# Holding the x transposes back behind the first chunk, in a one-core gated mix of linear attention and an MLP

## Chip, cores and metric

One core of one Trainium2 chip. The metric is device time in microseconds (us), the median of five runs. TensorE does the matmuls into PSUM, VectorE (DVE) and ScalarE (ACT) evacuate PSUM and do elementwise work, GpSimd (POOL) does masks and small copies, and SyncE (SP) issues nearly all DMAs.

## The reference

`x` is 2048 tokens by 640 features, everything is bfloat16. One input `x` goes through two blocks, and a gate for each token mixes the results:

```python
g = sigmoid((x * gate_w).sum(-1, keepdims=True))
# A: linear attention, H = 32 heads of 20
q, k, v = heads(x @ wqkv)
pq, pk = phi(q), phi(k)                  # phi(t) = where(t > 0, t + 1, exp(t)) + 1e-6
kv, z = einsum(pk, v), pk.sum(over s)    # for each head
a = (pq @ kv) / (pq . z + 1e-6) @ wo
# B: shifted mixer and MLP
h = gelu(layernorm(x) @ w1)
x1 = x + shifted(h) @ w2                 # four column groups, shifted by 1, -1, 2, -2 tokens
b = x1 + gelu(layernorm(x1) @ w3) @ w4   # 640 -> 1728 -> 640
out = g * a + (1 - g) * b
```

## The kernel before, in words

The instructions are written in a fixed order (`tc.manual_schedule()`): each engine runs its own instructions in program order, waiting on semaphores where data or buffers require it. A DMA instruction reuses one of eight DMA semaphores in turn, so it also waits until the DMA eight before it has landed. PSUM is handed out as four pairs of banks (`pair()`), in turn.

Tokens lie in 16 chunks of 128 (`NCH`) and 4 tiles of 512 (`NT`); 640 features are 5 groups of 128 (`DC`). TensorE's stages are, in order: K (L187, for each chunk 5 feature groups by 2 halves, 10 matmuls), q (L244), g (L321, k against x), W1 for tiles 0 and 1 with the small attention matrices between (L355, L374, L259, L388), W2 of tile 0 (L437), W1 of tiles 2 and 3, and then for each tile W3 (L484) with the next tile's W2 (L437) and this tile's attention (L468) woven in, followed by W4 (L517), whose sums go out with L531 and L536.

**The start.** K needs `xT`, which is x with features on partitions, and `wk_sb`, the weight rows for K. Loads go out on two queues, SP's and ACT's (L129 to L136): x chunk 0, the gate vector, K's weight rows 1, 0, 3, 2, 4 and x chunk 1. Chunks 0 and 1 are transposed on TensorE by `turn(c)` (L209 to L223): matmuls against an identity into PSUM, and then copies to `xT` on DVE (L220). The transposes of chunk 0 come in two groups, features 0 and 1, then 2 to 4. A column for the gate is made the same way (L219, L223) and sits as column 640 of `wk_sb`. Chunks 2 to 15 of `xT` come by DMA transposes from DRAM, written right behind the weight loads on SP's queue (L137, L138; `load_xT`, L124), in pieces of 1, 1, 2, 2, 4 and 4 chunks. After them, on the same queue: the weights for q (L139), the rest of x (L140, L141), the weights for v (L142), w1 (L143), six pieces of wo (L145), w2 in eight pieces (L147, L148) and w3 (L149).

While nothing has arrived, TensorE runs matmuls on constants ("fillers", `warmup`, L200). Chunk 0 of K takes the feature groups in the order 1, 0, 3, 4, 2 (`k0_order`), with a filler of 256 columns before the second and the third, and `turn(1)` before the fourth (L227 to L232). The copies of L171 (GpSimd, 20 of them) build `w1x` out of `w1_sb`.

**Scaling q.** `scale_t(t)` (L278 to L280) multiplies tile t of `pqT`, the 5 x 512 columns of phi(q), by the reciprocal denominators `rb`, on DVE. It needs `rb` (four DMAs, L276), and the attention matmuls of that tile (L468) need it. Tiles 0 and 1 are scaled before W1 of tile 3 in DVE's order, tiles 2 and 3 after it (L589 to L594).

**W4.** `w4_tile(t)` (L547) runs W4's matmuls of token chunks 0 and 2, then the rest rows and W3's rest of the next tile, then chunks 1 and 3; DVE adds the results up (L531) and SP stores them.

Of the kernel before, what the change touches and what calls it, by code (L numbers as in the profile page):

```python
# [16 lines left out]
def kernel(  # L17
# [13 lines left out]
    nc = tc.nc  # L31
    P = 128
    S, D = A_x.shape[1], A_x.shape[2]
# [6 lines left out]
    DC = D // P  # L40
# [4 lines left out]
    CG = D // 4  # L45
# [4 lines left out]
    NG = 6  # L50
    row0 = [g * GW for g in range(5)] + [D - P]
# [5 lines left out]
    wqkv_v = A_wqkv.rearrange("(c p) f -> p c f", p=P)  # L57
# [13 lines left out]
    def pair():  # L71
        return ps.tile([P, 2, 512], F32, name="pp")
# [5 lines left out]
    w1_sb = const.tile([P, DC, D], BF16)  # L78
    w1x = const.tile([P, DC, P], BF16)
    w2_sb = const.tile([P, DC, D], BF16)  # L80
    w3_sb = const.tile([P, DC, F], BF16)
    wo_sb = const.tile([P, NG, D], BF16)
# [22 lines left out]
    wq_sb = hsT[:, :, 0:D]  # L105
    wv_sb = m_sb
# [5 lines left out]
    xT = st1.tile([P, DC, S], BF16)  # L112
# [5 lines left out]
    sp, aq, gq = nc.sync, nc.scalar, nc.gpsimd  # L118

    def load_x(c0, c1, q=sp):  # L120
        q.dma_start(x_sb[:, c0:c1, 0:D], x2[c0 * P:c1 * P, :].rearrange("(c p) d -> p c d", p=P))  # L121

    def load_xT(c0, c1):
        sp.dma_start_transpose(xT[:, :, c0 * P:c1 * P], x2[c0 * P:c1 * P, :])  # L124

    def load_wk(q, dc):
        q.dma_start(wk_sb[:, dc, 0:D], A_wqkv[dc * P:(dc + 1) * P, D:2 * D])  # L127
# [6 lines left out]
    load_wk(sp, 3)  # L134
    load_wk(aq, 2)
    load_wk(sp, 4)  # L136
    for c0, c1 in ((2, 3), (3, 4), (4, 6), (6, 8), (8, 12), (12, 16)):  # L137
        load_xT(c0, c1)  # L138
    sp.dma_start(wq_sb, wqkv_v[:, :, 0:D])  # L139
    load_x(2, 8)  # L140
    load_x(8, 16)  # L141
    sp.dma_start(wv_sb[:], wqkv_v[:, :, 2 * D:3 * D])  # L142
    sp.dma_start(w1_sb[:], B_w1.rearrange("(c p) f -> p c f", p=P))  # L143
    for g in range(NG):
        sp.dma_start(wo_sb[:, g, :], A_wo[row0[g]:row0[g] + P, :])  # L145
    for g in range(4):
        sp.dma_start(w2_sb[:, g, :], B_w2[CG * g:CG * g + P, :])  # L147
        sp.dma_start(w2_sb[32 * g:32 * (g + 1), 4, :], B_w2[CG * g + P:CG * (g + 1), :])  # L148
    sp.dma_start(w3_sb[:], B_w3.rearrange("(c p) f -> p c f", p=P))  # L149


    nc.gpsimd.memset(mhalf[:], -0.5)
# [10 lines left out]
    for m, n, off in ((bmask, GH, 0), (bmask5, 2, 88)):  # L163
# [2 lines left out]
                                base=-off, pattern=[[-Dh, n], [0, 4]], channel_multiplier=1)  # L166
        nc.gpsimd.affine_select(out=m[:], in_=m[:], compare_op=ALU.is_ge, fill=0.0,
                                base=off + Dh - 1, pattern=[[Dh, n], [0, 4]], channel_multiplier=-1)
    for dc in range(DC):
        for g in range(4):  # L170
            nc.gpsimd.tensor_copy(w1x[:, dc, 32 * g:32 * (g + 1)], w1_sb[:, dc, CG * g + P:CG * (g + 1)])  # L171


    def phi(dst, src, n):
# [8 lines left out]
    def k_mm(pt, c, dcs, first=0, last=DC - 1):  # L183
        for dc in dcs:
            for hf in range(2):
                n = HD + hf
                nc.tensor.matmul(pt[:, hf, 0:n], lhsT=xT[:, dc, c * P:(c + 1) * P],  # L187
                                 rhs=wk_sb[:, dc, hf * HD:hf * HD + n], start=(dc == first), stop=(dc == last))
# [9 lines left out]
    def warmup(n, w=TS):  # L198
        for i in range(n):
            nc.tensor.matmul(warm[:, 1, 0:w], lhsT=one[:, 0:P], rhs=one[:, 0:w], start=True, stop=True)  # L200
# [8 lines left out]
    def turn(c):  # L209
        for pt, a, b in turns:  # L210
            ptb = pt[:, 0, :].bitcast(BF16) if c else pt[:, 0, :]
            for dc in range(a, b):
                dst, src = ptb[:, (dc - a) * P:(dc - a + 1) * P], x_sb[:, c, dc * P:(dc + 1) * P]
                if c:
                    nc.tensor.transpose(dst, src, ident[:])
                else:
                    nc.tensor.matmul(dst, lhsT=src, rhs=ident[:], start=True, stop=True)
            if c == 0 and b == DC:
                nc.tensor.matmul(pt[:, 1, 0:DC], lhsT=g5z[:], rhs=ident[:, 0:DC], start=True, stop=True)  # L219
            nc.vector.tensor_copy(xT[:, a:b, c * P:(c + 1) * P],  # L220
                                  ptb[:, 0:(b - a) * P].rearrange("p (c s) -> p c s", c=b - a))
            if c == 0 and b == DC:
                nc.vector.tensor_copy(wk_sb[:, :, D], pt[:, 1, 0:DC])  # L223

    turn(0)
    warmup(1, TS)
    for n, dc in enumerate(k0_order):  # L227
        if n == 3:
            turn(1)
        elif 1 <= n < 3:  # L230
            warmup(1, 2 * P)
        k_mm(kp, 0, (dc,), first=k0_order[0], last=k0_order[-1])  # L232
    k_evac(kp, 0)
    for c in range(1, NCH):
# [43 lines left out]
    def scale_t(t):  # L278
        sl = pqT[:, :, t * TS:(t + 1) * TS]
        nc.vector.tensor_tensor(sl, sl, rb[:, t:t + 1, :].broadcast_to([P, DC, TS]), op=ALU.mult)  # L280
# [177 lines left out]
    def x1_scale(t, cc):  # L458
        c = t * CPT + cc
        x1 = st[t]["x1"][cc]  # L460
        nc.scalar.activation(x1[:], x1[:], ACT.Copy, scale=omg[:, c:c + 1])
# [27 lines left out]
    def w3_rest(t, dst):  # L489
        for dc in range(DC):  # L490
            for v in range(2):
                nc.tensor.matmul(dst[FR * v:FR * (v + 1), :], lhsT=w3_sb[:, dc, FF * P:F],  # L492
                                 rhs=st[t]["lnT"][:, dc, v * LT:(v + 1) * LT], start=(dc == 0), stop=(dc == DC - 1))
        st[t]["h2x"] = h2x_p.tile([P, LT], BF16, name="h2x")
        nc.scalar.activation(st[t]["h2x"][:], dst, ACT.Gelu_apprx_tanh)  # L495
# [3 lines left out]
    def w4_tiles(t, ccs, pts):  # L499
        if t < NT - 1:  # L500
            for cc in ccs:
                pt = pair()
                pts[cc, 0], pts[cc, 1] = (pt[:, 0, TS - LT:TS], 0, LT), (pt[:, 1, 0:D - LT], LT, D)
                pts[cc, "rest"] = pt[:, 0, 0:LT]
                pts[cc] = pt[:].rearrange("p h e -> p (h e)")[:, TS - LT:TS - LT + D]
        else:
            for _ in range(3 if 0 in ccs else 1):
                pts["pairs"] = pts.get("pairs", []) + [pair()]
            homes = {0: (0, 1), 2: (1, 2)} if 0 in ccs else {1: (3, 3), 3: (2, 0)}
            for cc, (w, n) in homes.items():  # L510
                wide, narrow = pts["pairs"][w][:, 0, :], pts["pairs"][n][:, 1, 0:NW]
                pts[cc, 0], pts[cc, 1] = (narrow, 0, NW), (wide, NW, D)

    def w4_mm(t, cc, pts, hf, start):
        dst, a, b = pts[cc, hf]
        for fc in range(FF):
            nc.tensor.matmul(dst, lhsT=st[t]["h2"][:, fc * TS + cc * P:fc * TS + (cc + 1) * P],  # L517
                             rhs=w4_sb[:, fc, a:b], start=start and fc == 0, stop=not start and fc == FF - 1)

    def w4_rest(t, pts):  # L520
        for u in range(2):
            for hf in range(2):
                for v in range(2):
                    rows = slice(FR * v, FR * (v + 1))
                    dst, a, b = pts[u + 2 * v, hf]
                    nc.tensor.matmul(dst, lhsT=st[t]["h2x"][rows, u * P:(u + 1) * P],  # L526
                                     rhs=w4_sb[rows, FF, a:b], start=u == 1, stop=u == 0)
# [10 lines left out]
    def w4_out(t, cc, pts):  # L538
        oc = outp.tile([P, D], BF16, name="oc")
        if t < NT - 1:  # L540
            w4_stt(t, cc, oc, pts[cc], 0, D)
        else:
            for hf in range(2):
                w4_stt(t, cc, oc, *pts[cc, hf])
        w4_store(t, cc, oc, 0, D)

    def w4_tile(t):  # L547
        last = t == NT - 1
        pts = {}
        w4_tiles(t, (0, 2), pts)  # L550
        for cc in (0, 2):
            if not last:
                x1_scale(t + 1, cc)
            for hf in (1, 0):
                w4_mm(t, cc, pts, hf, True)
        w4_tiles(t, (1, 3), pts)
        w4_rest(t, pts)
        if not last:
            w3_rest(t + 1, pts[0, "rest"])
        for cc in (0, 2):  # L560
            w4_out(t, cc, pts)
        ocs = {}
        for cc, hf in ((1, 1), (3, 1), (1, 0), (3, 0)) if last else ((1, 0), (1, 1), (3, 0), (3, 1)):
            if not last and hf == 0:
                x1_scale(t + 1, cc)
            w4_mm(t, cc, pts, hf, False)
            if last:
                if hf == 1:
                    ocs[cc] = outp.tile([P, D], BF16, name="oc")
                w4_stt(t, cc, ocs[cc], *pts[cc, hf])  # L570
                w4_store(t, cc, ocs[cc], *pts[cc, hf][1:])
            elif hf == 1:
                w4_out(t, cc, pts)
# [13 lines left out]
    nc.sync.dma_start(w4_sb[0:FR, FF, :], B_w4[FF * P:F, :])  # L587
    nc.sync.dma_start(w4_sb[FR:P, FF, :], B_w4[FF * P:F, :])
    scale_t(0)  # L589
    scale_t(1)  # L590
    for fcs in w1_split:
        w1_unit(3, fcs)
    scale_t(2)
    scale_t(3)  # L594
    for cc in range(CPT):
        x1_scale(0, cc)
    NW3 = (FF + 1) // 2
# [45 lines left out]
```

## Time and profile before

| | us |
|---|---|
| median of five runs | 263.57 (263.08 to 266.35) |
| the profiled execution's own time | 263.57 |
| its span, first to last instruction | 261.9 |
| busy: TensorE | 257.5 |
| busy: DVE, ACT, GpSimd | 142.0, 83.0, 18.7 |
| K's unbroken run of matmuls starts | 6.66 |
| q starts | 27.80 |
| last output add starts | 259.19 |

The profile is of one execution; the times in it count from the span's start. "Busy" of TensorE is the union of its matmuls, whose ends are modelled. The chain of waits is followed back from the last instruction; each step in it is what the next one waited for. A row of a timeline gives start, length, engine, line, operation, output and inputs, and in brackets the idle time before it with what ended it. An issue on SP ("SPq") lasts as long as SP is busy with it; the data land later.

### The profile page before, as it was taken

To read this page: it belongs to the slowest core of one execution; us is meant where nothing else is said; L and a number is where in the kernel's file an instruction comes from. 1 tells how busy PE (TensorE), PEld (TensorE's weight loads), DVE (VectorE), ACT (ScalarE), POOL (GpSimd) and SP (SyncE) were. 2 spreads that over 40 slices of the span, in tenths; PEclk is the share of its full clock that TensorE was granted. 3 is DMA by queue.
4 is the path that set the end of the run, shared out by engine and by line. 5 is a ranking of instruction groups with operands and counts; after the bars stand their busy time and mean duration, and the time that the engine had idled before them with its cause. 6 is when DMAs were issued, how large, how long until landed. Compare 5 with 4: busy or idle time off the path is not lost.

```text
span 261.9 us, 4141 instructions
## 1 busy us (share of the span) xinstructions
PE 257.5 (98%) x1670; PEld 158.7 (61%) x1670; DVE 142.0 (54%) x277; ACT 83.0 (32%) x124; POOL 18.7 (7%) x64
## 2 busy tenths in 40 slices
PE   7999999999999999999999999999999999999995
PEld 3777555688854644565676555577565577555553
DVE  2688778799947884898203465403456603112132
ACT  1555454321165446531511212412131322142100
POOL 3000040012220140001000001000001000000000
PEclk9999999999999999999999999999999999999999
DMA  7999987016656726990402000502000401100011
GB/s 196 202 205 376 363 232 298 0 28 122 124 109 76 222 58 139 179 290 13 87 3 75 25 3 0 100 3 75 28 0 1 85 18 50 53 0 0 0 53 50
DMA packets 47265, 25.78 MB, mean 98 GB/s; under 512 B 35214, under 2 KB 46478, under 8 KB 47246
## 3 DMA queue, kind: packets, MB, share of 16 engines
q1 hardware_dynamic: 46804, 25.03, 37.6%
q10 hardware_dynamic: 442, 0.49, 0.5%
q8 instruction: 13, 0.21, 0.3%
q14 instruction: 6, 0.05, 0.1%
HBM read 13.03 MB, written 3.60 MB: 64 GB/s over the span
## 4 chain that ended last, share of the span: by engine, by line
PE 96%; DMA 2%; SPq 0%; DVE 0%; issue 0%
PE pp L517 22%; PE pp L484 21%; PE pp L468 8%; PE pp L321 8%; PE pp L437 8%; PE pp L355 8%; PE pp L244 8%; PE pp L187 8%; DMA wk_sb<-in_A_wqkv_dram 2%; PE pp L492 1%; PE pp L526 1%; PE pp L388 1%; PE pp L374 1%; PE pp L259 0%; SPq L127 0%; SPq L121 0%
## 5 line engine op out<-in xcount | busy, mean ns | idle before, releaser
L484 PE MATMUL pp<-lnxT,w_sb 128*128 128x512 bf16 x260 | 60.4, 379 | 0.0
L517 PE MATMUL pp<-w_sb,h 128*128 128x384 bf16 (+3 forms) x416 | 57.9, 299 | 0.0
L486 ACT ACTIVATE h<-pp 128x1024 bf16<-128x1024 f32 (+1 forms) x28 | 27.0, 963 | 82.2 <-PE pp L484 82.2
L517 PEld LDWEIGHTS <-h 128*128 128x128 bf16 x416 | 38.3, 98 | 19.3 <-issue 1.1
L531 DVE SCALAR_TENSOR_TENSOR oc<-pp,omg,x 128x640 bf16<-128x640 f32 (+2 forms) x20 | 14.4, 748 | 51.4 <-ACT h2x L495 27.6
L484 PEld LDWEIGHTS <-w_sb 128*128 128x128 bf16 x260 | 25.4, 98 | 26.8
L471 DVE SCALAR_TENSOR_TENSOR x<-pp,gate,x 128x640 f32<-128x640 f32 x16 | 13.9, 867 | 20.4 <-PE pp L468 20.4
L179 ACT ACTIVATE e<-pp 128x640 bf16<-128x640 f32 (+1 forms) x26 | 21.5, 827 | 9.6 <-PE pp L244 9.6
L468 PE MATMUL pp<-m_sb,pqT 128*128 128x320 bf16 x160 | 24.3, 299 | 0.0
L437 PE MATMUL pp<-w_sb,hsT 128*128 128x320 bf16 x160 | 23.9, 299 | 0.0
L187 PE MATMUL pp<-wk_sb,xT 128*128 128x320 bf16 (+1 forms) x160 | 22.6, 299 | 0.8 <-DMA wk_sb<-in_A_wqkv_dram 0.3
L321 PE MATMUL pp<-x_sb,pk 128*128 128x320 bf16 (+1 forms) x160 | 22.0, 300 | 0.0
L244 PE MATMUL pp<-xT,hsT 128*128 128x512 bf16 x100 | 21.7, 379 | 0.0
L440 DVE TENSOR_TENSOR x<-pp,x_sb 128x640 f32<-128x640 f32 x16 | 13.0, 813 | 15.7 <-PE pp L437 15.6
L321 PEld LDWEIGHTS <-pk 128*128 128x128 bf16 x160 | 18.8, 118 | 3.2
L437 PEld LDWEIGHTS <-hsT 128*128 128x128 bf16 x160 | 15.7, 98 | 8.0
L468 PEld LDWEIGHTS <-pqT 128*128 128x128 bf16 x160 | 15.7, 98 | 7.8
L187 PEld LDWEIGHTS <-xT 128*128 128x128 bf16 x160 | 15.6, 98 | 7.1 <-issue 0.8
L355 PE MATMUL pp<-lnxT,w_sb 128*128 128x512 bf16 x80 | 18.1, 379 | 0.0
L244 PEld LDWEIGHTS <-hsT 128*128 128x128 bf16 x100 | 11.8, 118 | 9.7
L291 POOL TENSOR_SCALAR rstd<-mv 128x4 f32<-128x4 f32 (+1 forms) x11 | 3.4, 312 | 153.7 <-DVE mv L297 153.7
L181 DVE SCALAR_TENSOR_TENSOR pk<-pp,e 128x640 bf16<-128x640 f32 x16 | 13.2, 825 | 1.7
(75 smaller groups left out, 186.3 us busy)
## 6 DMA issues: line engine op xcount, KB each, us to landing
out_dram<-oc SPq DMA_DIRECT2D x14, 160.0 KB, 1.8
w_sb<-in_B_w_dram SPq DMA_DIRECT2D x1, 2160.0 KB
w_sb<-in_B_w_dram SPq DMA_DIRECT2D x1, 2080.0 KB, 12.1
x_sb<-in_A_x_dram SPq DMA_DIRECT2D x1, 1280.0 KB
x_sb<-in_A_x_dram SPq DMA_DIRECT2D x1, 960.0 KB, 7.5
wo_sb<-in_A_wo_dram SPq DMA_DIRECT2D x6, 160.0 KB, 7.8
m_dram<-mst SPq DMA_DIRECT2D x2, 480.0 KB, 3.7
hsT<-in_A_wqkv_dram SPq DMA_DIRECT2D x1, 800.0 KB
```

The lines of the kernel that those rows point to most:

```text
L179: nc.scalar.activation(ev, src, ACT.Exp)
L187: nc.tensor.matmul(pt[:, hf, 0:n], lhsT=xT[:, dc, c * P:(c + 1) * P], rhs=wk_sb[:, dc, hf * HD:hf * HD + n], start=(dc == first), stop=(dc ...
L244: nc.tensor.matmul(pt[:, t % 2, :], lhsT=wq_sb[:, dc, :].rearrange("p (m j) -> p j m", j=DC)[:, j], rhs=xT[:, dc, t * TS:(t + 1) * TS], st ...
L321: nc.tensor.matmul(pt[:, hf, 0:HD + hf], lhsT=w, rhs=x_sb[:, c, hf * HD:(hf + 1) * HD + hf], start=(c == 0), stop=(c == NCH - 1))
L355: nc.tensor.matmul(pt[:, i, :], lhsT=w, rhs=lnxT[t][:, dc, :], start=(dc == 0), stop=(dc == DC - 1))
L437: nc.tensor.matmul(pt[:, hf, 0:HD], lhsT=hsT[:, fc, 2 + c * P:2 + (c + 1) * P], rhs=w2_sb[:, fc, hf * HD:(hf + 1) * HD], start=(fc == 0), ...
L468: nc.tensor.matmul(pt[:, hf, 0:HD], lhsT=pqT[:, j, c * P:(c + 1) * P], rhs=m_sb[:, j, hf * HD:(hf + 1) * HD], start=(j == 0), stop=(j == D ...
L471: nc.vector.scalar_tensor_tensor(x1, pt[:, :, 0:HD], gate[:, c:c + 1], x1, op0=ALU.mult, op1=ALU.add)
L484: nc.tensor.matmul(pt[:, k, :], lhsT=w3_sb[:, dc, fc * P:(fc + 1) * P], rhs=lnT[:, dc, :], start=(dc == 0), stop=(dc == DC - 1))
L486: nc.scalar.activation(h2[:, 2 * i * TS:(2 * i + n) * TS], pt[:].rearrange("p h e -> p (h e)")[:, 0:n * TS], ACT.Gelu_apprx_tanh)
L517: nc.tensor.matmul(dst, lhsT=st[t]["h2"][:, fc * TS + cc * P:fc * TS + (cc + 1) * P], rhs=w4_sb[:, fc, a:b], start=start and fc == 0, stop ...
L531: nc.vector.scalar_tensor_tensor(oc[:, a:b], src, omg[:, c:c + 1], st[t]["x1"][cc][:, a:b], op0=ALU.mult, op1=ALU.add)
```

## The change

- The loads behind the weight rows on SP's queue, from `load_xT` on, are put into a function `late_loads()` that is called after `turn(0)`. In `turn(0)`, DVE now writes one column of `xT`, feature group 0, at the first token of chunk 2. The DMA transpose of chunk 2 overwrites it and so waits on SP for that memset; everything behind it on SP's queue waits with it.
- The transposes are cut into pieces of 1, 1, 1, 1, 1, 1, 2, 2 and 4 chunks instead of 1, 1, 2, 2, 4 and 4.
- In `turn(0)` the gate column's matmul and its copy into `wk_sb` come after the first group of features, no longer after the second; the memset follows that copy, before the second group's copy on DVE.
- The two 256-column fillers between K's first pieces are taken out.
- The four 128-row loads of w2 become one; its four 32-row loads follow.
- The 20 copies of `w1x` stand after `late_loads()` in the program; GpSimd's own order stays as it was.
- `scale_t(0)` stays where it was. Tiles 1, 2 and 3 are scaled at the head of `w4_tile(0)`, `w4_tile(1)` and `w4_tile(2)`, in DVE's order after the last attention add of the tile and before W4's first output add.

```diff
-    for c0, c1 in ((2, 3), (3, 4), (4, 6), (6, 8), (8, 12), (12, 16)):
-        load_xT(c0, c1)
-    sp.dma_start(wq_sb, wqkv_v[:, :, 0:D])
...
-    for g in range(4):
-        sp.dma_start(w2_sb[:, g, :], B_w2[CG * g:CG * g + P, :])
-        sp.dma_start(w2_sb[32 * g:32 * (g + 1), 4, :], B_w2[CG * g + P:CG * (g + 1), :])
-    sp.dma_start(w3_sb[:], B_w3.rearrange("(c p) f -> p c f", p=P))
+    def late_loads():
+        for c0, c1 in ((2, 3), (3, 4), (4, 5), (5, 6), (6, 7), (7, 8), (8, 10), (10, 12), (12, 16)):
+            load_xT(c0, c1)
+        sp.dma_start(wq_sb, wqkv_v[:, :, 0:D])
...
+        sp.dma_start(w2_sb[:, 0:4, :], B_w2.rearrange("(g c) f -> c g f", g=4)[0:P])
+        for g in range(4):
+            sp.dma_start(w2_sb[32 * g:32 * (g + 1), 4, :], B_w2[CG * g + P:CG * (g + 1), :])
+        sp.dma_start(w3_sb[:], B_w3.rearrange("(c p) f -> p c f", p=P))
...
-            if c == 0 and b == DC:
+            if c == 0 and a == 0:
                 nc.tensor.matmul(pt[:, 1, 0:DC], lhsT=g5z[:], rhs=ident[:, 0:DC], start=True, stop=True)
...
-            if c == 0 and b == DC:
+            if c == 0 and a == 0:
                 nc.vector.tensor_copy(wk_sb[:, :, D], pt[:, 1, 0:DC])
+                nc.vector.memset(xT[:, 0:1, 2 * P:2 * P + 1], 0.0)
 
     turn(0)
+    late_loads()
...
         if n == 3:
             turn(1)
-        elif 1 <= n < 3:
-            warmup(1, 2 * P)
         k_mm(kp, 0, (dc,), first=k0_order[0], last=k0_order[-1])
...
     def w4_tile(t):
         last = t == NT - 1
         pts = {}
+        if not last:
+            scale_t(t + 1)
         w4_tiles(t, (0, 2), pts)
...
     scale_t(0)
-    scale_t(1)
     for fcs in w1_split:
         w1_unit(3, fcs)
-    scale_t(2)
-    scale_t(3)
```

More of the change, by code (lines that the diff above doesn't have):

```diff
@@ L136 @@
     load_wk(sp, 4)
-    for c0, c1 in ((2, 3), (3, 4), (4, 6), (6, 8), (8, 12), (12, 16)):
-        load_xT(c0, c1)
[L139 to L145, printed above, removed]
-    for g in range(4):
-        sp.dma_start(w2_sb[:, g, :], B_w2[CG * g:CG * g + P, :])
-        sp.dma_start(w2_sb[32 * g:32 * (g + 1), 4, :], B_w2[CG * g + P:CG * (g + 1), :])
-    sp.dma_start(w3_sb[:], B_w3.rearrange("(c p) f -> p c f", p=P))
+    def late_loads():
+        for c0, c1 in ((2, 3), (3, 4), (4, 5), (5, 6), (6, 7), (7, 8), (8, 10), (10, 12), (12, 16)):
+            load_xT(c0, c1)
+        sp.dma_start(wq_sb, wqkv_v[:, :, 0:D])
+        load_x(2, 8)
+        load_x(8, 16)
+        sp.dma_start(wv_sb[:], wqkv_v[:, :, 2 * D:3 * D])
+        sp.dma_start(w1_sb[:], B_w1.rearrange("(c p) f -> p c f", p=P))
+        for g in range(NG):
+            sp.dma_start(wo_sb[:, g, :], A_wo[row0[g]:row0[g] + P, :])
+        sp.dma_start(w2_sb[:, 0:4, :], B_w2.rearrange("(g c) f -> c g f", g=4)[0:P])
+        for g in range(4):
+            sp.dma_start(w2_sb[32 * g:32 * (g + 1), 4, :], B_w2[CG * g + P:CG * (g + 1), :])
+        sp.dma_start(w3_sb[:], B_w3.rearrange("(c p) f -> p c f", p=P))
     nc.gpsimd.memset(mhalf[:], -0.5)
@@ L168 @@
                                 base=off + Dh - 1, pattern=[[Dh, n], [0, 4]], channel_multiplier=-1)
-    for dc in range(DC):
-        for g in range(4):
-            nc.gpsimd.tensor_copy(w1x[:, dc, 32 * g:32 * (g + 1)], w1_sb[:, dc, CG * g + P:CG * (g + 1)])
     def phi(dst, src, n):
@@ L221, in turn @@
                                   ptb[:, 0:(b - a) * P].rearrange("p (c s) -> p c s", c=b - a))
-            if c == 0 and b == DC:
+            if c == 0 and a == 0:
                 nc.vector.tensor_copy(wk_sb[:, :, D], pt[:, 1, 0:DC])
+                nc.vector.memset(xT[:, 0:1, 2 * P:2 * P + 1], 0.0)
     turn(0)
+    late_loads()
+    for dc in range(DC):
+        for g in range(4):
+            nc.gpsimd.tensor_copy(w1x[:, dc, 32 * g:32 * (g + 1)], w1_sb[:, dc, CG * g + P:CG * (g + 1)])
     warmup(1, TS)
```

## The prediction

> **What bounds the kernel now.** I read the page first, its busy row and its chain, to see which engine the time belongs to.
>
> ```profile
> PE 257.5 (98%) x1670; PEld 158.7 (61%) x1670; DVE 142.0 (54%) x277; ACT 83.0 (32%) x124; POOL 18.7 (7%) x64
> ...
> PE 96%; DMA 2%; SPq 0%; DVE 0%; issue 0%
> ```
>
> TensorE fills the span and is 96% of the chain that ended last; DMA is 2%. Only what shortens or interrupts TensorE's own stream counts. So next the chain in order of time, for the one place where it is not TensorE:
>
> ```profile
> 1.71 0.42 SPq L127
> 2.14 0.04 issue
> 2.18 4.44 DMA wk_sb<-in_A_wqkv_dram
> 6.62 0.04 issue
> 6.66 21.14 PE pp L187 x154
> 27.80 21.58 PE pp L244 x100
> ```
>
> The whole start hangs on the load of K's weight rows dc 4 (issued 2.18, landed 6.62). From 6.66 on K runs 154 matmuls back to back, and q follows at once. Then the timeline of TensorE's first pieces of K:
>
> ```profile
> 4.15 0.31 PE L187 MATMUL pp<-wk_sb,xT 128*128 128x320 bf16 x1
> 4.70 0.30 PE L187 MATMUL pp<-wk_sb,xT 128*128 128x321 bf16 x1 [0.24 <-DVE wk_sb L223]
> 4.84 0.27 PE L200 MATMUL pp<-const-bfloat16-1.0 128*128 128x256 bf16 x1
> 4.94 0.43 PE L187 MATMUL pp<-wk_sb,xT 128*128 128x320 bf16 x2
> 5.21 0.27 PE L200 MATMUL pp<-const-bfloat16-1.0 128*128 128x256 bf16 x1
> 5.81 0.43 PE L187 MATMUL pp<-wk_sb,xT 128*128 128x320 bf16 x2 [0.32 <-DMA wk_sb<-in_A_wqkv_dram]
> ```
>
> Pieces 1 and 0 are early; both 256-column fillers stand in front of the wait that ends with wk rows 3 at 5.77. Last SP's own timeline, for the transposes:
>
> ```profile
> 1.25 1.37 SPq L127 DMA_DIRECT2D wk_sb<-in_A_wqkv_dram  x3
> 2.66 13.35 SPq L124 DMA_TRANSPOSE xT<-in_A_x_dram  x6
> 16.05 0.58 SPq L139 DMA_DIRECT2D hsT<-in_A_wqkv_dram  x1
> ```
>
> Six transposes keep SP issuing for 13.35 us. Taken apart by narrower windows: one chunk 1.30 and 1.28 us, two chunks 1.71 and 1.41, four 3.87 and 3.56. The semaphore updates of the trace give the landings: wk rows 1 at 3.99, 0 at 4.30, 3 at 5.77, x chunk 1 at 6.00, wk rows 4 at 6.62 and 2 at 6.82; the transposes at 7.46 (chunk 2), 8.00 (3), 9.72 (4, 5), 11.72 (6, 7), 15.81 (8 to 11), 18.03 (12 to 15). K takes 1.362 us a chunk: chunk 1 starts at 7.20, 2 at 8.57, 8 at 16.74, 12 at 22.19.
>
> **Holding the transposes back: what it can free.** The gain would be earlier weight loads. The packet records speak against much of it. The transposes' 256-byte packets first appear at 5.3 us, because on SP's queue they stand behind the weight loads; by then wk rows 1, 0 and all but the last of rows 3 and x chunk 1 have their data. What they can disturb is the tail: 15 of 16 parts of wk rows 4 had landed by 5.90, and the last, on one engine that had fallen behind, at 6.62; rows 2 show data packets nearly done at 5.9, yet all their 16 updates come at 6.67 to 6.82. The hold ends late enough to help only a little. DVE's first cast starts at 3.67 and its follower started 0.34 later; the 5-column copy (169 ns) and the new one-column memset (nearest row: the 112 ns memset of L202) follow, so the memset ends near 4.26 and SP starts chunk 2 near 4.3 instead of 2.66. A transpose from SBUF (L313, L325) shows its first packets about 1.1 us after its issue starts, so these begin near 5.4: as before, within 0.1 us. The late engine's weight packets come first either way. Bounds: 0, if the late engine is late by itself; and 0.7 us, if descriptor generation for the transposes was slowing the loads: from 3.0 to 5.5 us 640 packets of 1280 bytes started, against some 154 per 0.5 us later (770), so 130 packets or 0.42 us, plus up to 0.3 us of rows 2 and 4 waiting for their updates. Nearer to the first: **-0.2 us**.
>
> **The copies that change places.** The gate column copy now comes before the second cast, so the 0.24 us wait at 4.70 goes; but it stands before the wait for wk rows 3 (5.81) and is worth 0. The second cast (548 ns) starts near 4.25 instead of 4.01 and ends near 4.8; the third piece needs it at 5.81, so 1.0 us covers it. Cost 0.
>
> **No fillers.** Two matmuls of 256 columns (start to start 0.11 us each) lie before an idle stretch that ends with a DMA: removing them gives 0. Here a rule speaks against the change. The Trainium skill, "TensorE: Matmul & The Clock Gate", Part 1, says that an idle window of about 3.4 us drops the array to half rate until a busy window has passed. The trace shows the two rates: the first 512-column fillers start 0.43 us apart (1.21, 1.64, 2.06), in W1 50 matmuls take 10.79 us, 0.216 each; the granted clock column says 1.00 at both. Without fillers the longest gap is from about 4.6 to 5.81, 1.2 us. By the gap the loss is 0; if a thinner window is enough to fall back, 3.4 us at half rate lose 1.7 us. Taken: **0**, the gap being a third of the window.
>
> **Chunk by chunk, and later.** SP starts 1.65 us later. It issues six single chunks (1.30 each and 0.04 between), two pairs (1.56, the mean of 1.71 and 1.41) and one four (3.56 to 3.87): (8,10) starts at 4.3 + 6 x 1.34 = 12.3, (10,12) at 13.9, (12,16) at 15.5, and SP is free near 19.2 instead of 16.0. A second rule speaks against it, "DMA: Bandwidth & Descriptors", Rules for kernel authors: coalesce many small transfers. The rows agree in kind (two singles 2.6 us, a pair 1.56). By the rule the later chunks come too late and the 3.2 us show up as a stall; by the rows they use up slack. Landings: singles 2.6 to 3.7 us after their start (SBUF ones take 2.4; chunk 3 took 4.0 with a jam before it), so chunk 2 at 6.9 to 8.0 against 8.57, and every later single keeps that margin, since 1.34 us of issue stands against 1.362 of K. The pair (8,10): 3.7 us (most of its parts) to 4.64 (all of (6,8)) after its start, 16.0 to 16.9, against 16.74 less what the start gained. The four: 5.6 to 7.3 us, 21.1 to 22.8 against 22.19. Stall between 0 and 0.7; nearest to the undisturbed rows: **+0.1 us**.
>
> **Queued behind them on SP.** wq, x, wv, w1, wo, w2, w3 move by up to 3.2 us. wq landed at 21.58 and would at 24.8, needed by q at 27.64: 2.8 us of cover, after which each us costs one. x (27.7) is needed by the g units at 49.2, w1 (32.3) on TensorE at 71.2, wv at 76.6, w2 at 86.4, w3 (45.6) at 102.6. GpSimd's 20 copies of w1x move with w1; its next work waits for statistics until 56.3. Four w2 issues become one, about 1 us less on SP. All 0.
>
> **Scaling q in W4.** Four scales of 1.49 us, in this place:
>
> ```profile
> 105.40 2.89 DVE L280 TENSOR_TENSOR pqT<-pqT,rb 128x2560 bf16<-128x2560 bf16 x2 [4.07 <-DMA m_sb<-m_dram]
> ...
> 109.41 2.90 DVE L280 TENSOR_TENSOR pqT<-pqT,rb 128x2560 bf16<-128x2560 bf16 x2
> 112.22 0.82 DVE L440 TENSOR_TENSOR x<-pp,x_sb 128x640 f32<-128x640 f32 x1
> ...
> 126.63 0.89 DVE L471 SCALAR_TENSOR_TENSOR x<-pp,gate,x 128x640 f32<-128x640 f32 x1 [1.59 <-PE pp L468]
> 137.21 1.68 DVE L531 SCALAR_TENSOR_TENSOR oc<-pp,omg,x 128x640 bf16<-128x640 f32 x2 [9.70 <-ACT h2x L495]
> ```
>
> Three leave: 3 x 1.49 = 4.5 us before 112.22, where W2's first evacuation was late (its matmuls had ended at 106.15). TensorE paid 70 ns for that at 112.9, from the starts of its matmuls. Each goes to where DVE idles 9.7 us at the head of W4; its queue there holds only output adds at 137, and its user, the attention matmuls of the next tile, starts at 153. Without that cover it would cost 1.5 us a tile. **-0.07 us**.
>
> **Sum** on the profiled execution (span 261.9; its own time 263.57, 1.67 outside the span, and equal to the median of the five): -0.2 + 0 + 0.1 - 0.07 = -0.17, rounded to -0.2: 263.4 us.
>
> **Rivals.** (a) *The loads do speed up*: the dips in the packet rate are the transposes' doing, the late engine disappears, 0.7 us at the start, less a stall of 0.1 at chunk 8: 262.9. For it: 128 instead of 154 packets per 0.5 us. Against: no transpose packet before 5.3. (b) *Late chunks, slower than before*: the pair (8,10) or the four lands after K reaches chunk 8 or 12. It decides once (8,10) takes over 4.4 us or (12,16) over 6.7 from issue to landing; at the worst rows (4.64; 7.28) K stands 0.2 + 0.45 us: 264.2 without any gain. For it: those rows; against: they had other transposes jammed around them. (c) *Clock falls back*: +1.7, 265.1. (d) *Nothing moves*: the forecast's gains and stalls are each 0: 263.6.
>
> **How the numbers follow.** Forecast with (d), which it cannot be told from: 0.53, own range 263.1 to 263.8. (a) 0.21, (b) 0.17, (c) 0.06, others 0.03. The range leaves out (c), the far ends of (a) and (b) and an odd run: 262.3 to 264.5. A measurement here tells 1%, 2.6 us, from no change. No case reaches that alone: faster 0.03, same 0.93, slower 0.04 (clock loss together with late chunks).
>
> **What would show it.** Chunk 2's transpose issued near 4.3; K's unbroken run starting at 6.3 to 6.7; no wait for transposes in TensorE's row before 27.7, at most one near 16.6 or 22; K ending by 27.7; no wait of L468 near 113; scales inside DVE's idle stretches. Wrong if K's run starts before 6.2 (a), if TensorE waits over 0.3 us on transposes (b), or if K's chunks take over 1.4 us each (c).

## The result, and the profile after

The changed kernel takes 264.21 us (median of 42 runs, 263.68 to 265.28) against 263.46 for the kernel before (80 runs): a ratio of 1.0026, interval 1.0018 to 1.0034. It became 0.7 us slower, where 0.2 us of gain was forecast. The profiled execution has a span of 262.5 us and an own time of 264.21, so span and time grew together (0.6 and 0.64).

On the page, TensorE's share of the chain is the first thing that has changed: 96% before, 93% now. The other rows are of the same page: the busy times, a DMA queue (packets, MB, share of the DMA engines), and K's group (its last column is the idle time before its matmuls and what ended most of it).

```profile
PE 257.8 (98%) x1668; PEld 158.8 (60%) x1668; DVE 142.3 (54%) x278; ACT 83.0 (32%) x124; POOL 18.7 (7%) x64
...
q8 instruction: 13, 0.21, 0.3%
...
PE 93%; SPq 3%; DMA 2%; DVE 1%; issue 0%
...
L185 PE MATMUL pp<-wk_sb,xT 128*128 128x320 bf16 (+1 forms) x160 | 22.8, 304 | 1.1 <-DMA xT<-in_A_x_dram 0.7
```

K now waits for a transpose. The chain in order of time says for which one:

```profile
3.70 0.42 DVE xT L218
...
4.69 0.88 SPq L124
...
12.21 5.17 DMA xT<-in_A_x_dram
17.43 11.07 PE pp L185 x80
28.50 21.58 PE pp L245 x100
```

Before, this chain hung on wk rows 4 up to 6.62 and on TensorE after that. Now it runs through DVE's casts, then SP's row of held transposes, then one transpose that was issued at 12.21 and took 5.17 us: the pair of chunks 8 and 9. Only at 17.43 does TensorE take over, and q starts at 28.50 instead of 27.80. TensorE's timeline shows the same hole:

```profile
6.44 10.25 PE L185 MATMUL pp<-wk_sb,xT 128*128 128x320 bf16 x74
17.43 11.07 PE L185 MATMUL pp<-wk_sb,xT 128*128 128x320 bf16 x80 [0.75 <-DMA xT<-in_A_x_dram]
```

By the starts of the matmuls: chunk 1 of K starts at 6.98 (before 7.20), chunk 8 at 17.43 instead of 16.51, which is where 6.98 + 7 x 1.362 would put it. So -0.22 at the start, +0.91 at chunk 8, and -0.07 for the wait of L468 that is gone: +0.62, the span's 0.6. There is no second place.

The forecast's issue times came out within 0.4 us. SP's timeline, and DVE's around the hold:

```profile
4.26 15.30 SPq L124 DMA_TRANSPOSE xT<-in_A_x_dram  x9
19.61 0.58 SPq L140 DMA_DIRECT2D hsT<-in_A_wqkv_dram  x1
```
```profile
4.04 0.17 DVE L221 CAST wk_sb<-pp 128x5 bf16<-128x5 f32 x1
...
4.16 0.06 DVE L222 MEMSET xT<- 128x1 bf16 x1
...
128.06 1.48 DVE L281 TENSOR_TENSOR pqT<-pqT,rb 128x2560 bf16<-128x2560 bf16 x1
137.84 1.68 DVE L532 SCALAR_TENSOR_TENSOR oc<-pp,omg,x 128x640 bf16<-128x640 f32 x2 [8.30 <-ACT h2x L496]
```

The memset ends at 4.22 and the first transpose is issued at 4.26; the pair starts at 12.21 and SP is free for the next load at 19.61. The scale of tile 1 (128.06) lies where DVE still has 8.3 us to spare.

**What sits in the hole.** Queue 8 of the page carries 13 packets of 16 KB, of kind instruction. TensorE's row has 1668 matmuls and as many weight loads, 3336 instructions, one packet for every 257. By the starts in the trace, TensorE begins 220 to 304 instructions between one packet and the next, 255 on average. That these packets bring TensorE's instructions is an inference from these counts. The packet records put the first of them at 15.28, 1.10 us long, just as the last of the pair's own packets start. Packets of 256 bytes (the transposes' own) that start in each 0.2 us from 15.0 on:

```
15.0 226   15.2 154   15.4 135   15.6  77   15.8  77   16.0  95   16.2  78
16.4  23   16.6   8   16.8   8   17.0   7   17.2 173   17.4 226   17.6 225
```

About 226 is what undisturbed transposes reach here. From 15.2 to 17.2 the transposes crawl and almost stand, and then resume. The stage table (length, busy time and count of PE, PEld, DVE, ACT and POOL, granted clock, DMA share, GB/s) shows that from 16 to 17 the DMA engines had packets under way all the time (a share of 1.03; packets overlap, so it can pass 1) and yet moved only 54 GB/s:

```profile
15.00:16.00 1.00, 1.00 (x10) 0.71 (x8) 0.90 (x2) 0.64 (x2) 0.00 (x0) 1.00 1.28 188
16.00:17.00 1.00, 0.68 (x6) 0.27 (x3) 0.79 (x3) 0.41 (x3) 0.00 (x0) 1.00 1.03 54
17.00:18.00 1.00, 0.57 (x5) 0.42 (x6) 0.79 (x3) 0.49 (x1) 0.00 (x0) 1.00 0.97 214
```

A transfer counts as landed when all its 16 semaphore updates have come. Of the pair's, five came at 15.86 to 15.99, one at 16.20, and ten only at 17.26 to 17.38. The kernel before has the same event: its packet is at 13.74, at the end of the transpose of chunks 8 to 11, with 11 updates at 14.32 to 14.46 and five at 15.68 to 15.81. There K wanted chunk 8 only at 16.74, and nothing had to wait for it.

### The profile page after: what moved, and what is told of

Its sections match the earlier page's. It is cut to its first block, busy times and chain, and to the rows that moved or that the text cites. A ratio compares the mean times of both kernels' runs of the same rounds, so it can differ in the third digit from the quotient of the medians.

```text
span 262.5 us, 4140 instructions
## 1 busy us (share of the span) xinstructions
PE 257.8 (98%) x1668; PEld 158.8 (60%) x1668; DVE 142.3 (54%) x278; ACT 83.0 (32%) x124; POOL 18.7 (7%) x64
## 4 chain that ended last, share of the span: by engine, by line
PE 93%; SPq 3%; DMA 2%; DVE 1%; issue 0%
PE pp L518 22%; PE pp L485 21%; PE pp L322 8%; PE pp L438 8%; PE pp L469 8%; PE pp L356 8%; PE pp L245 8%; PE pp L185 4%; SPq L124 3%; DMA xT<-in_A_x_dram 2%; PE pp L493 1%; PE pp L198 1%; PE pp L527 1%; PE pp L389 1%; PE pp L375 1%; PE pp L260 0%
## 5 line engine op out<-in xcount | busy, mean ns | idle before, releaser
L472 DVE SCALAR_TENSOR_TENSOR x<-pp,gate,x 128x640 f32<-128x640 f32 x16 | 13.9, 867 | 20.7 <-PE pp L469 20.7
```

Source lines behind the costliest of these rows:

```text
L472: nc.vector.scalar_tensor_tensor(x1, pt[:, :, 0:HD], gate[:, c:c + 1], x1, op0=ALU.mult, op1=ALU.add)
```

## The experiments

The theory: the hold is the whole loss; it takes 1.6 us of lead from the transposes, and a packet of instructions that used to fall into that lead now stands on K's path. Its rivals: the finer cuts keep SP busy longer, so the pair is late whatever the hold does; or the missing fillers cost time. And for the start: did the hold bring K forward at all? Each expectation was written before its run and says in its own words what the theories give. Ratios are against the kernel before on the same chip.

### Which part costs the time

**No hold.** The memset is gone and `late_loads()` is called where the loads stood before; all the rest is as changed.

```diff
+    late_loads()
...
-                nc.vector.memset(xT[:, 0:1, 2 * P:2 * P + 1], 0.0)
...
     turn(0)
-    late_loads()
```

> The changed kernel without the memset and with the later loads issued where they were before; all else as changed (cuts chunk by chunk, no fillers, scaling in W4). Theory: no wait at chunk 8, since all transposes are issued 1.6 us earlier; K's run starts within 0.25 us of either kernel; 263.3 to 263.5 us, at or a little under the kernel before. Rival (fillers or scaling cost the time): 264.1 to 264.3.

263.32 us, 1.0005 (0.9987 to 1.0022). SP issues the transposes from 2.66 on again. TensorE's timeline:

```profile
6.62 21.14 PE L186 MATMUL pp<-wk_sb,xT 128*128 128x320 bf16 x154 [0.29 <-DMA wk_sb<-in_A_wqkv_dram]
```

The nine cuts stay and cost nothing: K runs its 154 matmuls unbroken. Issued at 10.60, the pair landed at 14.74, 4.1 us later; the packet came at 15.28 again and held the next pair up to 17.54, which K wants at 19.4. The finer cuts are not the cause.

**The hold alone.** The kernel before with the hold, with the order of the gate column that goes with it, the six old cuts, the fillers, the old loads of w2, and the old place of the scaling. Against the changed kernel:

```diff
-        for c0, c1 in ((2, 3), (3, 4), (4, 5), (5, 6), (6, 7), (7, 8), (8, 10), (10, 12), (12, 16)):
+        for c0, c1 in ((2, 3), (3, 4), (4, 6), (6, 8), (8, 12), (12, 16)):
...
+        elif 1 <= n < 3:
+            warmup(1, 2 * P)
...
-        if not last:
-            scale_t(t + 1)
...
+    scale_t(1)
...
+    scale_t(2)
+    scale_t(3)
```

> The kernel before with the hold alone (memset, later loads after it, the gate column first), with its own cuts of 1, 1, 2, 2, 4 and 4 chunks, its fillers and its scaling. The start gains 0.1 to 0.25 us as in the changed kernel. Theory (the hold uses up the slack of 0.9 us that the four-chunk piece had at chunk 8): the piece is issued near 9.9 and lands 5.9 to 7.3 us later, 15.8 to 17.2, against a need of 16.5; 263.2 without and 264.0 with the wait. Rival (the finer cuts are the loss, the hold is free): 263.2.

263.99 us, 1.0018 (1.0001 to 1.0036): by the medians 0.6 us over the 263.37 beside it. Chunks 8 to 11 were issued at 10.06 and landed at 16.83. In the profiled execution K began late, with chunk 1 at 7.37, and wanted them at 16.91, so no wait for a transpose is to be seen in it; with the start of the kernel before (chunk 8 at 16.74) there would be one of 0.1 us. Of the 0.35 us by which its span exceeds that of the kernel before, 0.17 are the late start and 0.17 more lie in front of the attention matmuls at 113. The price stands, but the interval only just leaves out no change, and this trace does not show the price as a wait of K.

**The fillers back**, the rest as changed:

```diff
         if n == 3:
             turn(1)
+        elif 1 <= n < 3:
+            warmup(1, 2 * P)
```

> The changed kernel with the two 256-column fillers back. Theory: they lie before a wait for weights; 264.2 us, no change, unless they move the instruction fetch (4 instructions earlier, some 0.3 us). Rival (without the fillers TensorE stays at half rate longer: in the changed profile the first six matmuls of K start 0.27 us apart, in the one before 0.14): the full rate returns and the start gains 0.3 to 0.5 us: 263.8.

264.19 us, 1.0039 (1.0024 to 1.0053): no change against the changed kernel, and the same chain:

```profile
12.20 5.18 DMA xT<-in_A_x_dram
```

On the same chip the version without the hold (and without these fillers) took 263.32, so the hold costs 0.87 us here.

**Only the scaling moved**, everything else as before.

```diff
-    scale_t(1)
...
-    scale_t(2)
-    scale_t(3)
...
+        if not last:
+            scale_t(t + 1)
```

> The kernel before with only the scaling of tiles 1 to 3 moved into W4. Theory: the 70 ns wait at the first attention matmul near 113 goes, nothing else moves: 263.4 us, a ratio of 0.9997 to 1. Rival (the later parts of the change cost part of the loss): over 263.7.

263.44 us, 1.0004 (0.9996 to 1.0012), beside 263.41. The 70 ns in front of L468 at 112.9 are gone from the trace (112.95 follows its predecessor at once), and such a size is below what the runs can tell.

**Did the hold bring K forward?** Two kernels in which K needs no transpose: chunks 2 to 15 of K read the columns of chunks 0 and 1, once with the hold and once without.

```diff
-                nc.tensor.matmul(pt[:, hf, 0:n], lhsT=xT[:, dc, c * P:(c + 1) * P],
+                nc.tensor.matmul(pt[:, hf, 0:n], lhsT=xT[:, dc, (c % 2) * P:(c % 2 + 1) * P],
```

> The changed kernel, but K's chunks 2 to 15 read the columns of chunks 0 and 1 again (K and the gate are those of other tokens), so that K does not wait for any DMA transpose. It measures the start alone, with the hold. If the hold frees the weight loads as the one profile shows (K's run 0.2 us earlier): 0.15 to 0.3 us under the twin without the hold. If that was one execution's chance: the same within 0.1 us. Either way the 0.91 us of chunk 8 are gone: 263.2 to 263.5.

> The twin: the changed kernel without the hold, with K's chunks 2 to 15 reading the columns of chunks 0 and 1. As without the hold before, since no chunk waited there: 263.3 to 263.5 us. The difference of the two is what the hold is worth at the start, with nothing behind it to take it back.

With the hold 263.29 us, 1.0002 (0.999 to 1.0015); without it 263.29, 1.0004 (0.9988 to 1.0021). Chunk 1 of K starts at 6.96 with it and at 6.94 without, q at 27.56 and 27.54. The 0.22 us that the one profile of the changed kernel showed at its start come just as well without a hold. The intervals, 0.3 to 0.4 us either way, leave room for a small gain; nothing in the runs shows one. And with K free of the transposes the hold costs nothing that these runs show: its price is the wait.

### What makes the pair late

**The pair cut in two singles**, so that chunk 8 has less in front of it.

```diff
-        for c0, c1 in (..., (7, 8), (8, 10), (10, 12), (12, 16)):
+        for c0, c1 in (..., (7, 8), (8, 9), (9, 10), (10, 12), (12, 16)):
```

> The changed kernel with the pair of chunks 8 and 9 moved as two single chunks. Theory (the hold costs 0.9 us at chunk 8, because the pair is complete only 5.2 us after its issue, at 17.38): singles before it completed 2.8 to 3.0 us after their issue, so chunk 8 lands near 15.2 and K reaches it at 16.5 without a wait; 263.3 to 263.7 us, the rest depending on the four-chunk piece, issued about 1.0 us later. Rival (TensorE lost its clock early, and the later parts cost the rest): 264.2, the wait at chunk 8 is only moved. Rival (the 16 KB instruction fetch near 15.3 holds up whatever transpose is then under way): a wait of 0.5 us or more at chunk 8, 9 or 10 stays, about 264.

264.41 us, 1.0043 (1.0027 to 1.0059). A miss for the theory, which had K run through, and what the second rival had said: chunk 8 landed in time, and the wait went two chunks further:

```profile
6.37 12.97 PE L185 MATMUL pp<-wk_sb,xT 128*128 128x320 bf16 x94
19.87 8.35 PE L185 MATMUL pp<-wk_sb,xT 128*128 128x320 bf16 x60 [0.53 <-DMA xT<-in_A_x_dram]
```

The packet started at 15.13. The single of chunk 9 landed 4.1 us after its issue (the seven before it 2.8 to 2.9), and the pair behind it at 19.82, 5.0 us after. Here the transpose that was in transfer when the packet came is late, and so is its follower.

**A plain load behind the pair.** A fifth of the weights for q (160 KB, no transpose) is put between the pair (8, 10) and the pair (10, 12); in a second kernel another fifth behind (10, 12) as well.

```diff
             load_xT(c0, c1)
-        sp.dma_start(wq_sb, wqkv_v[:, :, 0:D])
+            if c0 == 8:
+                sp.dma_start(wq_sb[:, 0:1], wqkv_v[:, 0:1, 0:D])
+        sp.dma_start(wq_sb[:, 1:DC], wqkv_v[:, 1:DC, 0:D])
```

> The changed kernel with one plain load (a fifth of q's weights, 160 KB) between the pairs (8,10) and (10,12) on SP's queue, instead of after all transposes. Theory A (the pair's data are in by about 15.3, and its completion is held because the next transpose's writes stand still): with plain writes behind it the pair completes near 16.0, K does not wait at chunk 8; (10,12) lands 0.6 to 1.0 us later, near 19, close to its need at 19.1; 263.2 to 263.7. Theory B (the pair's own data or writes are late): the wait at chunk 8 stays at 0.7 us or more and chunk 10 waits too; 264.2 to 264.8.

> The changed kernel with a fifth of q's weights loaded between (8,10) and (10,12), and another between (10,12) and (12,16). With one such load the pair (8,10) completed at 15.98 instead of 17.38, but (10,12) then fell to the instruction fetch and completed at 19.76, against a need near 19.2 when K starts as in the changed profile. With plain writes behind both pairs, (10,12) should complete near 18.3 and K run through; the four-chunk piece moves 0.5 us later, to about 22.5 against 22.0. 263.2 to 263.5 if K runs through; 263.5 to 263.9 if the wait only moves to chunk 12.

The first took 263.53 us, 1.0002 (0.9981 to 1.0023), the second 264.0, 1.002 (1.0011 to 1.0029), where K had been expected to run through or to wait at chunk 12. Their edits are alike up to the pair. In the traces the packet came at different times, and K began 1.03 us later in the first:

| | packet starts | the pair's 16 updates | from issue | K waits at chunk 8 |
|---|---|---|---|---|
| changed kernel | 15.28 | 5 to 15.99, 1 at 16.20, 10 at 17.26 to 17.38 | 5.2 us | 0.91 us |
| one plain load | 17.58 | all at 15.82 to 15.98 | 3.8 us | none |
| two plain loads | 15.29 | 15 at 15.87 to 16.03, 1 at 17.53 | 5.3 us | 1.18 us |

TensorE's timeline, first of the kernel with one load, then of the one with two:

```profile
7.35 21.14 PE L187 MATMUL pp<-wk_sb,xT 128*128 128x320 bf16 x154
```
```profile
6.31 10.25 PE L187 MATMUL pp<-wk_sb,xT 128*128 128x320 bf16 x74
17.58 11.07 PE L187 MATMUL pp<-wk_sb,xT 128*128 128x320 bf16 x80 [1.02 <-DMA xT<-in_A_x_dram]
```

This is the clearest sign of the packet's part, though of one execution each: with the packet elsewhere the pair takes 3.8 us, with the packet at its end one update comes 1.5 us after the other fifteen. What stands behind seems to matter too. With a plain load there, one update is late; with a transpose there, ten in the changed kernel, but between 2 and 16 over all the profiles in which a transpose met a packet, so the count is not settled by these two. The kernel with one load is two-sided: in the profiled execution (264.3 us) K began late, chunk 1 at 7.89, since wk rows 3 landed at 6.5, so the absent wait owes something to that; of its 14 runs eight lie at 263.28 to 263.54 and six at 263.91 to 265.29. It is not a version that beats the kernel before.

**Sixteen more TensorE instructions early** (eight matmuls of 64 columns ahead of K's first chunk), meant to bring the packet about 1.1 us forward, off the pair's end.

```diff
     warmup(1, TS)
+    warmup(8, 64)
```

> The changed kernel with 8 more short fillers (64 columns, 16 TensorE instructions with their weight loads) in the idle stretch ahead of K. They should bring TensorE's first 16 KB instruction fetch, which started at 15.28 us between the pairs (8,10) and (10,12), forward by about 1.1 us of K's pace. Theory A (the fetch holds one DMA engine for 1.1 us, the transposes then under way wait for it, and the finished pair's completion waits behind them): the fetch falls before (8,10), and the wait at chunk 8 shrinks from 0.91 to 0.4 us or less; 263.3 to 263.8. Theory B (the pair as such is late, whatever is fetched): wait unchanged, 264.2.

264.22 us, 1.0026 (1.0013 to 1.0039): a miss. In its profile the packet started at 15.53 and the pair took 5.3 us, landing at 17.54. K had begun 1.06 us late (chunk 1 at 8.04) and wanted chunk 8 at 17.59. Measured from the start of chunk 1 the packet did come 0.8 us sooner (7.5 us after it instead of 8.3), but the run can't separate this from the late start. Inconclusive.

### Moving the packets

**Thirty more TensorE instructions at the start.** The five constant matmuls of 512 columns become twenty of 128, which cover as many columns; once in the changed kernel, once in the kernel before.

```diff
-    warmup(5)
+    warmup(20, P)
```

> The changed kernel with the five first fillers of 512 columns cut into twenty of 128 columns: the same length, 30 TensorE instructions more ahead of K. The first instruction fetch should come about 2 us of K's pace earlier than 15.28, near 12 to 13, among the single chunks, which have 1.3 us to spare. Theory A: no wait at chunk 8 (0.2 us at most); the gain at the start stays: 263.1 to 263.4. Theory B: wait unchanged, 264.2.

> The kernel before with its five first fillers cut into twenty of 128 columns (30 TensorE instructions more, nothing else). In the changed kernel this cost 1.4 us: the fetch came at 72.35, while the transposes of the g units (L326) were under way, one of them took 4.5 instead of 2.5 us, and TensorE waited 1.9 us at the kv unit (L375). If the place of the fetch alone does that, the kernel before loses as much: 265.2 to 265.8. If it took the hold or the finer cuts: 263.4.

In the changed kernel 265.61 us, 1.0079 (1.0053 to 1.0105), a miss by over 2 us. The packet came at 13.70 and K's wait moved from chunk 8 to chunk 7 (which starts at 15.58, 0.43 us behind the pace): three of that single's updates came at 15.47 to 15.53, the others around 13.9. The pair took 4.5 us and was in time. Yet the kernel is 1.4 us slower than the changed one. Its chain, first at chunk 7, then at the small attention matrices:

```profile
10.88 4.66 DMA xT<-in_A_x_dram
15.58 12.44 PE pp L185 x90
...
70.39 4.51 DMA wk_sb<-gs
...
75.72 2.58 DMA wk_sb<-gs
78.55 1.59 PE pp L375 x30
```

In the kernel before, which holds nothing back, the same edit gives 265.16 us, 1.0062 (1.005 to 1.0074), and its chain has this:

```profile
70.15 4.20 DMA wk_sb<-gs
...
78.06 1.59 PE pp L374 x30
```

The fourth packet now starts at 72.35 and 72.09. In both kernels without the edit it starts at 78.0 to 78.2, after the last of the g transposes. Here it meets the third last of them: 4.5 and 4.2 us from issue to landing instead of 2.6. ACT fills that buffer again only then (at 75.00 and 74.45), so the last transpose is late, and the small attention matrices (L375, L374) wait for it, 1.75 and 1.46 us by TensorE's timeline. Where these packets fall against a row of transposes is worth over a microsecond without any hold.

**The packet brought forward by many tiny matmuls** (32 rows by 32 columns): 44 in place of the five constant matmuls, and in a second kernel, whose lines are shown, two of the five kept and 28 tiny ones behind them.

```diff
+    def tiny(n):
+        for i in range(n):
+            nc.tensor.matmul(warm[0:32, 1, 0:32], lhsT=one[:, 0:32], rhs=one[:, 0:32], start=True, stop=True)
...
-    warmup(5)
+    warmup(2)
+    tiny(28)
```

> The changed kernel with its five first fillers replaced by 44 tiny ones (32 rows by 32 columns): 78 TensorE instructions more ahead of K, hold and cuts as changed. The first fetch should come some 5 us of K's pace earlier, near 8 to 11 us, and be over long before the pair (8,10). Theory A (fetch inside the pair's completion): the pair completes 3.8 to 4.2 us after its issue as where no fetch fell on it, near 16.2, and K does not wait at chunk 8; single chunks that meet the fetch may cost up to 0.5 us at chunk 4 to 6. Theory B (held pairs are late anyway): 5 us or more, and the wait at chunk 8 stays at 0.7 us or more. The whole time says little, since later fetches move too and may meet the transposes near 72 us.

> The same with two of the five fillers kept and 28 tiny ones (50 instructions more): the fetch should come some 3.4 us of K's pace earlier than 15.28. Theory A: the pair completes in 3.8 to 4.4 us and the wait at chunk 8 is gone or under 0.2 us; a wait of up to 0.6 us at chunk 5 to 7 instead. Theory B: the wait at chunk 8 stays at 0.7 us or more.

265.33 us, 1.0069 (1.005 to 1.0089), and 265.38, 1.0071 (1.0043 to 1.0099). The packets came at 11.84 and 11.92, ahead of the pair, and held the single of chunk 6 instead (4.5 and 4.7 us; 3.4 in the changed kernel). The pair behind still took 4.8 and 5.1 us, which fits neither theory: A had said at most 4.2 and 4.4, B a wait of 0.7 us or more. With 44 tiny matmuls K came to chunk 8 only at 18.20 and found the pair landed; with 28, K waited 0.16 us at chunk 6 and 0.32 at chunk 8:

```profile
17.32 11.07 PE L185 MATMUL pp<-wk_sb,xT 128*128 128x320 bf16 x80 [0.16 <-DMA xT<-in_A_x_dram]
```

The shorter wait is not the pair's doing: it landed at 17.28, only 0.10 us sooner than in the changed kernel, and K came to it 0.48 us later (0.31 from the start, the rest from chunk 6). The total times say nothing of it, because other prices came in. With 28 tiny matmuls the fourth packet again fell on the g transposes (70.78; one took 4.1 us, and TensorE waited 1.30 us). With 44 it came at 70.00 and was over before they began at 72.27; one of them took 3.25 us all the same, and TensorE waited 0.57 us there and stayed at half rate longer at the start (last section).

**The pair in all these profiles**, from issue to landing. Where no packet came during its transfer: 4.1 us (no hold) and 3.8 (one plain load). Where one came 0.3 us before its issue: 4.8 and 5.1 (tiny matmuls); 1.5 us after its issue: 4.5 (thirty instructions). Where one came 3.1 to 3.7 us after its issue, when its transfer was ending: 5.2 in the changed kernel, 5.2 (fillers), 5.3 (sixteen instructions), 5.3 (two plain loads), 5.9 and 6.1 (K freed, with and without the hold; the last with a packet of 1.61 us). The pairs of chunks 4 and 5 and of 6 and 7 in the kernels with six cuts, which met no packet, took 4.0 to 4.9 us, so only the last group stands clear of what a pair can take without one.

## Why the prediction was wrong

**Right.** The issue times of all nine transposes, wq's landing (24.81), the queue behind it, the copies that changed places, and the fillers at 0 (264.19 with them, 264.21 without). The nine finer cuts cost nothing by themselves (263.32 with them and without the hold). The clock: in the changed kernel TensorE had not reached full rate before the gap (K's matmuls are 0.27 us apart up to 5.85; full rate comes at about 6.0 us, and at 6.2 with the fillers), so that trace cannot show a fall. The kernel with one plain load, which has no fillers either, can. By their starts its matmuls are 0.14 us apart just before an idle stretch of 1.39 us and just after it:

```profile
4.22 0.90 PE L187 MATMUL pp<-wk_sb,xT 128*128 128x320 bf16 x4
6.51 0.43 PE L187 MATMUL pp<-wk_sb,xT 128*128 128x320 bf16 x2 [1.39 <-DMA wk_sb<-in_A_wqkv_dram]
```

So the reading of the Trainium skill, "TensorE: Matmul & The Clock Gate", Part 1, by the length of the gap held for a gap of this size. The scaling moved for -0.07 us in the trace. Two slips bear on nothing: rival (b)'s 0.45 us for the four chunks is 0.39 by its own starts, and the next tile's attention matmuls start at 154.47, not 153.

**The step that failed: "Stall between 0 and 0.7; nearest to the undisturbed rows: +0.1 us".** The stall is 0.91 us. The decision point of rival (b) was right: the pair decides once it takes over 4.4 us, and it took 5.17, landing 0.87 us after the 16.51 at which K's pace wanted it. But (b) was priced at 0.2 us for the pair, from a worst row of 4.64 us, and set aside because the slow rows "had other transposes jammed around them". The slowest of those, 7.28 us for chunks 8 to 11, was more than a jam: 11 of its 16 updates had come after 5.93 us, and the last five came 1.35 us later, after the instruction packet at 13.74. That was in the records of the kernel before, and slack hid it. Put on the pair, this gives an estimate from these two rows of 3.7 + 1.35 = 5.05 us, a stall of some 0.65; with the scaling's -0.07 and no gain at the start, 264.15 us. It is worked out after the result, and on a pair that met the packet as it did.

**The other: "-0.2 us" at the start.** Measured 0.0 (263.29 with the hold and without it, where K needs no transposes). The end of 0 that the prediction named was the true one: no transpose packet ran before 5.3 us, so there was little for the hold to keep away. Where K starts depends on which weight rows an execution gets late: chunk 1 started between 6.86 and 7.37 in most profiles, and near 8 in three, two of them with wk rows 3 late and one with the tiny matmuls.

**The mechanism, as far as it is shown.** The hold issues the transposes 1.6 us later while K starts where it did; that lead was the cover. This is shown by the kernel without a hold and by those with K freed; the one with the hold alone agrees in its time, not in its trace. That the pair's lateness is the packet's is shown by the changed kernel's own records and by the two kernels with plain loads, each in one execution; the single of chunk 9 in the first experiment on the pair agrees. Of the eleven profiles listed above, the six with the packet at the end of the pair's transfer are the six slowest. The late updates fit, in part, the Trainium skill, "DMA: Bandwidth & Descriptors", Queues, rings and completion order: each DMA engine takes its queues in turn, a whole packet at a time, and its increment of a semaphore lands only after all earlier writes of that engine, whichever queue they came from. By that rule a 1.1 us packet on one engine makes one update late, and the kernel with two plain loads has just that: one of 16, 1.5 us after the others. With a transpose behind, ten are late in the changed kernel, and nine of them the rule does not give. There the measurement decides: transposes as a whole nearly stop, until 0.8 us after the packet's end.

**Open.** Why transposes stand for so long after a packet. What sets its moment: in the kernel before with thirty more instructions the fourth packet came 6 us earlier, but the first not at all (13.99 against 13.74; TensorE had started about 195 instructions by then, against 161). And how much of the pair's 4.8 to 5.1 us behind an early packet is a jam handed on by the single before it: with 28 tiny matmuls the packet was over 1.05 us after the pair's issue, and the pair landed only 0.10 us sooner than in the changed kernel, so a packet need not stand at the pair's end for the pair to be late. No version was found that beats the kernel before: apart from the two with K freed, the best (no hold, only the scaling moved, one plain load), at 263.32 to 263.53, cannot be told from it.

## What to carry to other kernels

Before a load is held back, list not only when it must land but what already happens inside its slack: a late semaphore update in the old trace for which nobody waited becomes a wait once the slack is gone. Take the worst row apart by its updates (here eleven early, five late) before putting it down to a jam. And an edit that changes how many instructions an engine runs, fillers for instance, can shift its instruction packets anywhere after it, so a time that moves by 1 or 2 us need not have moved at the place of the edit.

## What the runs showed of the hardware

Packets of kind instruction, 16 KB each, took 0.88 to 1.61 us. Around the one at 15.28 the DMA transposes fell from 226 packets per 0.2 us to 77 and then to 8.

With 44 tiny matmuls in place of the five large ones, full rate came late in the one trace taken: K's matmuls were still spaced at half rate until 9.25 us (with five large ones until 3.5 to 6.7 us), and the same 154 matmuls took 22.42 us instead of 21.14, while the granted clock column stood at 1.00. The tiny ones also filled less time (until 2.17 us instead of 2.9), so the trace cannot separate their size from the time lost:

```profile
6.84 22.42 PE L185 MATMUL pp<-wk_sb,xT 128*128 128x320 bf16 x154
```
